# Attention and a bilinear feed-forward layer: the scaling of the second batch's sums of exponentials moves from VectorE to ScalarE

## The chip, the cores and the metric

The kernel runs on one core of a Trainium2 chip. The core has five engines that run their own queues of instructions in order and wait for one another through semaphores: TensorE (PE in the profile, with its weight loads as PEld), VectorE (DVE), ScalarE (ACT), GpSimd (POOL) and SyncE (SP), which here only issues DMAs. The metric is the time of one execution on the device in microseconds (us), lower is better. The median of three runs of the kernel before is 1006.17 us (1006.15 to 1007.19).

## The reference

Sliding-window attention over 8 batches, 8 heads, 576 positions and 64 channels per head is followed by a feed-forward layer that multiplies two projections with each other:

```python
scores = np.matmul(q, k.transpose(0, 1, 3, 2)) / np.sqrt(64)
bias = slopes[:, None, None] * (-np.abs(rel))        # rel = i - j
mask = (rel >= 0) & (rel < 128)
scores = np.where(mask, scores + bias, -1e9)
scores = scores - scores.max(axis=-1, keepdims=True)
attn = np.exp(scores)
attn = attn / (attn.sum(axis=-1, keepdims=True) + 1e-9)
x = (attn @ v)          # heads side by side: 4608 tokens x 512
out = ((x @ w_a) * (x @ w_b)) @ w_out      # 512 -> 1536 -> 512
```

All inputs and the output are float32.

## The kernel before

The float32 products are made of float16 ones: a matrix is scaled by a power of two and split into a high and a low float16 part, and three products (high by high, high by low, low by high) are added in PSUM. PE is therefore the engine with most of the work.

Attention goes by pairs of heads, four pairs to a batch, and a pair by nine blocks of 64 queries, which lie in four PSUM banks (`BANKS`). `scores` multiplies q and k of one bank on PE (L374 in the second batch, in plain float32; L378 in the later ones), adds the bias and takes the minimum on DVE (L382), and takes the exponential on ACT with its row sum (L383, into `sm`). `normalize` does this for the blocks that have been scored since the last call: it turns the sums into scaled reciprocals `rin` (one small instruction, L392 or L395, then the reciprocal on DVE, L396), and for each block multiplies the exponentials by `rin` and splits them into a high part on ACT (L399) and a low part on DVE (L400), both into `phl`. It is called twice for a pair, for 5 and 4 blocks or for 7 and 2. `transpose_probs` then transposes `phl` by a DMA that SP issues (L405), and `pv` multiplies it with v on PE (L501). ACT copies the result back over v (L414), and `split_x` (L435 on ACT, L436 on DVE) makes from it the float16 input `xs` of the feed-forward layer.

The first batch's attention has its own code (`first_attention`). The second batch's, `o.b == 1`, runs while PE does the first batch's feed-forward layer. From the third batch on, q and k are also scaled and split: squares on ACT (L321, with a row sum), the factor by way of DVE (L324, L336) and a small product on PE (`qtot`, L332), the split on ACT and DVE (L338, L339), then four DMAs on SP that lay the parts out (L347 to L350). The load of q and k of the pair after it (L311, L312) stands on SP behind these. There is one buffer for the loaded q and k, one for `phl` and one for the transposed probabilities `pT`.

The feed-forward layer of the first batch is `first_up` (the two projections, L836 on PE; copied by ACT at L783, multiplied by DVE at L785, split by ACT L829 and by DVE or POOL L830) and `first_down` (L812 on PE). `first_down` works in two halves of the tokens; each half adds up in four PSUM banks at a time, which ACT (L822) and DVE (L820) empty when it is complete, and the second half needs these banks. Five banks in all take turns. In the same time the weights are converted from float64: L131 and L133 on DVE, L130 on ACT and L135 on POOL, with squares on ACT (L141) and a sum over all partitions on PE (`wtot`, L101), after which ACT and DVE split the down weights (L230, L231).

What sets the order: the generators are woven together by `Pace` and `weave`, and a scheduler then orders the instructions of each engine by its own estimate of when each is ready, with some of them lifted by `high_priority`. SP's order is as written in the code everywhere. PE's is as written from the second batch's feed-forward layer on; in the first batch's it too comes from the scheduler. Once ordered, each engine takes its queue strictly from the front.

Of the kernel before, what the change touches and what calls it, by code (L numbers as in the profile page):

```python
# [17 lines left out]
AF = mybir.ActivationFunctionType  # L18
ALU = mybir.AluOpType
# [11 lines left out]
PSC = float(2.0**14)  # L31
# [15 lines left out]
def attention_then_bilinear_ffn(ctx: ExitStack, tc: tile.TileContext, qT, kT, vP, w_a, w_b, w_out, rel, slopes2, outT):  # L47
    nc = tc.nc
    vec, act, pe, pool, sp = nc.vector, nc.scalar, nc.tensor, nc.gpsimd, nc.sync
# [337 lines left out]
    def normalize(o):  # L387

        a, z = o.parts[0][0], o.n

        if o.b < 2:
            vec.tensor_scalar(out=o.rin[:, a:z], in0=o.sm[:, a:z], scalar1=1e-9, scalar2=1.0 / PSC, op0=ALU.add, op1=ALU.mult)  # L392
        else:

            act.activation(o.rin[:, a:z], o.sm[:, a:z], AF.Copy, scale=1.0 / PSC, bias=1e-9 / PSC)  # L395
        vec.reciprocal(o.rin[:, a:z], o.rin[:, a:z])  # L396
        for m, e, pc, w in o.parts:
            s = o.rin[:, m:m + 1]
            act.activation(phl[:, 0, pc:pc + w], e, AF.Copy, scale=s)  # L399
            vec.scalar_tensor_tensor(out=phl[:, 1, pc:pc + w], in0=e, scalar=s, in1=phl[:, 0, pc:pc + w], op0=ALU.mult, op1=ALU.subtract)  # L400
        o.parts = []
# [256 lines left out]
    def attention():  # L658
# [34 lines left out]
        for i in range(n + 1):  # L693
# [26 lines left out]
            if o and p != 2:  # L720
                with behind():
                    normalize(o)
# [7 lines left out]
            if two == 2 and p in (1, 3):  # L730
                if p == 2:
                    with behind():
                        normalize(o)
                scores(o, 3)
            yield i + 4 / 7
            if p == 2:
                prev.vhl = split_v(st, prev.p)
                if two == 1 or p not in (1, 3):
                    with behind():
                        normalize(o)  # L740
# [320 lines left out]
```

## Time and profile before

| | |
|---|---|
| median of the runs | 1006.17 us |
| the profiled execution's own time | 1006.95 us |
| its span in the trace | 1005.2 us |
| instructions | 23888 |
| PE idle or waiting, 100 to 200 us | 8.7 us |
| PE idle or waiting, 200 to 300 us | 2.7 us |
| DVE L396 | 56 instructions, from 66.9 to 860.7 us |

The span is what the trace covers; the execution's own time is some 1.8 us longer. The profile's page gives the busy time of each engine and the costliest groups of instructions. A line of the timeline gives start, duration, engine, line of the kernel, operation, output and inputs, and in brackets the idle time of the engine ahead of it with what ended that time. SPq stands for the issue of a DMA by SP.

### The profile page before, as it was taken

What the parts mean: (1) busy time and instruction counts of PE and PEld (TensorE: products, weight loads), DVE (VectorE), ACT (ScalarE), POOL (GpSimd) and SP (SyncE); (2) the same over time, 40 slices, a digit from 0 to 9 for tenths busy, and PEclk for the clock granted to TensorE, in tenths of its full rate; (3) what the DMA queues carried; (4) which work ended last, traced back from release to release, by engine and by line L of the source; (5) the groups of instructions that cost most, each with busy time, mean ns of one, the idle gap of its engine ahead of it and who ended that gap; (6) DMA issues with size and microseconds to landing.
All of it is one profiled execution on the core that took longest, in us unless ns stands there. A gap on an engine that the chain in (4) does not pass through costs nothing.

```text
span 1005.2 us, 23888 instructions
## 1 busy us (share of the span) xinstructions
PE 970.8 (97%) x9339; PEld 753.6 (75%) x9339; DVE 674.8 (67%) x1833; ACT 648.9 (65%) x1715; POOL 306.1 (30%) x345
## 2 busy tenths in 40 slices
PE   8789989999999999999999999999999999999998
PEld 5557656777777777777787777777777777777776
DVE  5888999557878566785768687666677576524530
ACT  7976779657767756767767767677666766413321
POOL 3533463104565321352226112220223022211100
PEclk9889999999999999999999999999999999999999
DMA  9317733564444442462624642474425632210001
GB/s 349 120 43 269 231 114 74 120 166 80 100 90 100 137 90 43 97 172 71 121 52 105 172 90 46 93 178 103 84 57 107 163 67 43 49 37 7 2 13 36
DMA packets 148433, 102.83 MB, mean 102 GB/s; under 512 B 120032, under 2 KB 128352, under 8 KB 147296
## 3 DMA queue, kind: packets, MB, share of 16 engines
q1 hardware_dynamic: 138816, 91.77, 37.2%
q10 hardware_dynamic: 9504, 9.54, 2.9%
q8 instruction: 73, 1.20, 0.5%
q14 instruction: 40, 0.33, 0.1%
HBM read 48.33 MB, written 9.44 MB: 57 GB/s over the span
## 4 chain that ended last, share of the span: by engine, by line
PE 70%; DVE 10%; ACT 4%; DMA 2%; issue 1%; POOL 1%; SPq 0%; ACTq 0%; DVEq 0%
PE dn_ps L932 19%; PE ch L836 19%; PE p L836 14%; PE up_ps L836 10%; PE x_ps L501 4%; PE sc_ps L378 3%; DVE phl L400 2%; PE dn_ps L812 2%; DMA v<-in_vP 1%; DVE t L382 1%; DVE xs L436 1%; ACT t L383 1%; DVE wup L150 1%; ACT phl L399 1%; DVE wup L257 1%
## 5 line engine op out<-in xcount | busy, mean ns | idle before, releaser
L836 PEld LDWEIGHTS <-wup 128*128 128x128 f16 x4224 | 409.1, 98 | 120.8 <-issue 14.3
L932 PE MATMUL dn_ps<-h,wdn 128*128 128x288 f16 x2016 | 254.3, 286 | 0.0
L932 PEld LDWEIGHTS <-wdn 128*128 128x128 f16 x2016 | 193.9, 98 | 51.7
L836 PE MATMUL ch<-xs,wup 128*128 128x288 f16 x1536 | 221.5, 286 | 0.8 <-ACT rc L861 0.6
L836 PE MATMUL up_ps<-xs,wup 128*128 128x288 f16 x1536 | 197.7, 288 | 5.8 <-DVE rc L785 4.2
L836 PE MATMUL p<-xs,wup 128*128 128x288 f16 x1152 | 172.6, 286 | 0.0
L891 POOL TENSOR_TENSOR rc<-rc,row 128x288 f32<-128x288 f32 x64 | 62.3, 974 | 278.8 <-DVE row L889 262.9
L400 DVE SCALAR_TENSOR_TENSOR phl<-t,rin,phl 128x192 f16<-128x192 f32 (+2 forms) x252 | 109.5, 474 | 19.0 <-ACT phl L399 18.8
L383 ACT ACTIVATE t<-t,mn 128x192 f32<-128x192 f32 (+2 forms) x252 | 107.2, 427 | 23.3 <-DVE mn L382 23.0
L829 ACT CAST h<-rc 128x576 f16<-128x576 f32 x96 | 64.2, 669 | 68.2 <-DVE rc L896 37.6
L399 ACT ACTIVATE phl<-t,rin 128x192 f16<-128x192 f32 (+2 forms) x252 | 88.7, 425 | 23.0 <-DMA pT<-phl 10.9
L830 DVE TENSOR_TENSOR h<-rc,h 128x576 f16<-128x576 f32 x90 | 71.1, 790 | 32.7 <-ACT h L829 32.0
L382 DVE CUSTOM_DVE_ANT_0 t<-sc_ps,bias,neg 128x192 f32<-128x192 f32 (+2 forms) x216 | 73.7, 389 | 7.8 <-PE sc_ps L378 7.7
L135 POOL TENSOR_TENSOR wup<-wup,wdn 128x512 int32<-128x512 int32 x36 | 54.6, 1539 | 44.6 <-DVE wup L133 14.6
L937 ACT ACTIVATE row<-dn_ps,oi 128x288 f32<-128x288 f32 x56 | 27.6, 494 | 56.7 <-PE dn_ps L932 56.5
L873 ACT ACTIVATE row<-ch,g 128x288 f32<-128x288 f32 x64 | 31.8, 497 | 50.1 <-PE ch L836 50.1
L436 DVE TENSOR_TENSOR xs<-v,xs 128x576 f16<-128x576 f32 x52 | 48.7, 950 | 21.7 <-ACT xs L435 21.5
L360 POOL TENSOR_SCALAR bias<-rel_sb,ninv,sl_sb 128x192 f32<-128x192 f32 x24 | 21.3, 887 | 123.5 <-DVE mn L382 123.5
L868 DVE TENSOR_TENSOR rc<-p,rc 128x288 f32<-128x288 f32 x64 | 29.1, 454 | 44.4 <-PE p L836 35.0
L896 DVE SCALAR_TENSOR_TENSOR rc<-rc,g,ch 128x288 f32<-128x288 f32 x64 | 32.6, 510 | 23.8 <-PE ch L836 23.6
L383 ACT ACTIVATION_READ_ACCUMULATOR t<-t,mn 128x1 f32 x252 | 47.7, 189 | 0.0
L430 POOL TENSOR_TENSOR xq<-xq,sq 128x576 bf16<-128x576 bf16 x22 | 29.6, 1345 | 56.8 <-ACT sq L429 56.7
(151 smaller groups left out, 1315.6 us busy)
## 6 DMA issues: line engine op xcount, KB each, us to landing
v<-in_vP SPq DMA_DIRECT2D x8, 1280.0 KB, 6.5
out<-row ACTq DMA_DIRECT2D x60, 144.0 KB, 1.8
qk<-in_qT SPq DMA_DIRECT2D x28, 288.0 KB, 3.9
qk<-in_kT SPq DMA_DIRECT2D x28, 288.0 KB, 4.4
wdn<-in_w_a SPq DMA_DIRECT2D x12, 512.0 KB, 4.5
wdn<-in_w_b SPq DMA_DIRECT2D x12, 512.0 KB, 5.6
wdn<-in_w_out SPq DMA_DIRECT2D x12, 512.0 KB, 4.3
qst<-qkh SPq DMA_DIRECT2D x24, 144.0 KB, 2.7
```

Of the source, the lines that this page charges most:

```text
L135: pool.tensor_tensor(out=t[:, m, :], in0=t[:, m, :], in1=low[:, m, :], op=ALU.add)
L382: vec.tensor_tensor_reduce(out=t[:, c:c + w], in0=ps[:, c:c + w], in1=o.bias[:, WIN - w:WIN], scale=-0.125 if o.b == 1 else o.neg, scalar= ...
L383: act.activation(t[:, c:c + w], t[:, c:c + w], AF.Exp, bias=o.mn[:, n:n + 1], scale=-1.0, accum_out=o.sm[:, n:n + 1])
L399: act.activation(phl[:, 0, pc:pc + w], e, AF.Copy, scale=s)
L400: vec.scalar_tensor_tensor(out=phl[:, 1, pc:pc + w], in0=e, scalar=s, in1=phl[:, 0, pc:pc + w], op0=ALU.mult, op1=ALU.subtract)
L436: vec.tensor_tensor(out=xs[:, n, 1, :, :], in0=src, in1=xs[:, n, 0, :, :], op=ALU.subtract)
L501: pe.matmul(xp[oc // 512][64 * h:64 * h + 64, o0:o0 + w], vt[0:rows, c:c + 64], probs(pt, rows, blocks, h), start=(n == 0 and first), stop ...
L829: act.copy(h[:, f, :, 0, :], hid)
L830: eng.tensor_tensor(out=h[:, f, :, 1, :], in0=hid, in1=h[:, f, :, 0, :], op=ALU.subtract)
L836: pe.matmul(ps[:, 0:HT], wup[:, a[0], a[1], wi, k, :], xs[:, b, xi, k, :], start=(first and n == 0), stop=(last and n == len(ks) - 1), ski ...
L891: pool.tensor_tensor(out=x0, in0=x0, in1=mid, op=ALU.mult)
L932: pe.matmul(ps[:, 0:HT], wdn[:, f, wi, e * P:(e + 1) * P], h[:, f, t, hi, :], start=(m == 0 and n == 0), stop=(m == NF - 1 and n == 2))
```

## The change

In `normalize` the branch for the first two batches goes. The second batch now scales its sums as the later ones do: ACT computes `sm / PSC + 1e-9 / PSC` in one instruction where DVE computed `(sm + 1e-9) / PSC`. (`normalize` is never called for batch 0.)

```diff
-        if o.b < 2:
-            vec.tensor_scalar(out=o.rin[:, a:z], in0=o.sm[:, a:z], scalar1=1e-9, scalar2=1.0 / PSC, op0=ALU.add, op1=ALU.mult)
-        else:
-
-            act.activation(o.rin[:, a:z], o.sm[:, a:z], AF.Copy, scale=1.0 / PSC, bias=1e-9 / PSC)
+
+        act.activation(o.rin[:, a:z], o.sm[:, a:z], AF.Copy, scale=1.0 / PSC, bias=1e-9 / PSC)
         vec.reciprocal(o.rin[:, a:z], o.rin[:, a:z])
```

The instructions are the same but for these eight. The order is not: from some 133 us on the scheduler lays out the rest of the first batch's feed-forward layer differently, up to about 215 us; SP's order stays as it was. In the changed file the lines behind the diff are 3 lower, so that L396, L399 and L400 read L393, L396 and L397, L414, L429 and L435 read L411, L426 and L432, and L783 and L829 read L780 and L826. Everywhere else in this text the lines are those of the kernel before.

On ACT, where the down weights are split (L230), the last two splits of the third pair of heads of the second batch (`phl`, L399 x2) stood right behind the twelfth L230:

```order
L230 ACTIVATE wdn<-wup,ratio 128x512 x11
L783 COPY rc<-up_ps 128x288
L230 ACTIVATE wdn<-wup,ratio 128x512
L399 ACTIVATE phl<-t,rin 128x192 x2
L414 ACTIVATE v<-x_ps 128x512
```

In the changed kernel, the place on ACT where they are now, thirteen instructions behind the last L230:

```order
L432 CAST xs<-v 128x576
L426 ACTIVATE sq<-v 128x576
L432 CAST xs<-v 128x576
L396 ACTIVATE phl<-t,rin 128x192 x2
L383 ACTIVATE t,sm<-t,mn 128x192 x2
L826 CAST h<-rc 128x2x288
L338 ACTIVATE qkh<-qk,own 128x1152
```

They have moved behind the second of two casts of x, and just ahead of the split of the third batch's first q and k (L338).

Next on ACT, a little later, the end of the fourth pair of the second batch: its last exponentials (L383 x2) and splits (L399 x4) stood ahead of the squares of the next loaded q and k (L321). Before:

```order
L414 ACTIVATE v<-x_ps 128x64
L429 ACTIVATE sq<-v 128x576
L383 ACTIVATE t,sm<-t,mn 128x192 x2
L399 ACTIVATE phl<-t,rin 128x192 x4
L321 ACTIVATE qkl,qs<-qk 128x1152
```

And in the changed kernel, the same place on ACT:

```order
L411 ACTIVATE v<-x_ps 128x64
L426 ACTIVATE sq<-v 128x576
L321 ACTIVATE qkl,qs<-qk 128x1152
L383 ACTIVATE t,sm<-t,mn 128x192 x2
L392 ACTIVATE rin<-sm 128x4
L396 ACTIVATE phl<-t,rin 128x192 x4
```

L321 is now ahead of them, with the added scaling (L392 here) among them.

The same place on DVE before, with the reciprocal and the low parts (L400) of that pair ahead of L324, which uses L321's sum, and then the first scores of the third batch:

```order
L396 RECIPROCAL rin<-rin 128x4
L400 SCALAR_TENSOR_TENSOR phl<-t,rin,phl 128x192 x4
L324 TENSOR_SCALAR both<-halves,qs 128x2
L382 ISA t,mn<-sc_ps,bias,neg 128x64
L382 ISA mn 128x1
```

In the changed kernel, DVE at the same place:

```order
L324 TENSOR_SCALAR both<-halves,qs 128x2
L393 RECIPROCAL rin<-rin 128x4
L397 SCALAR_TENSOR_TENSOR phl<-t,rin,phl 128x192
L382 ISA t,mn<-sc_ps,bias,neg 128x64
L382 ISA mn 128x1
L382 ISA t,mn<-sc_ps,bias,neg 128x128
L382 ISA mn 128x1
```

L324 now leads, and the four low parts are spread among the scores' instructions; on both engines the emptying of the down product's banks (L820, L822) still comes behind all of these.

## The prediction

> **What bounds the kernel now.** I read the page's busy shares first, then a table of stages, then the waits of PE.
>
> ```profile
> PE 970.8 (97%) x9339; PEld 753.6 (75%) x9339; DVE 674.8 (67%) x1833; ACT 648.9 (65%) x1715; POOL 306.1 (30%) x345
> ```
> ```profile
> 100.00:200.00 100.00, 91.31 (x864) 67.40 (x862) 87.22 (x211) 76.79 (x187) 40.66 (x32) 0.97 0.51 137
> 200.00:300.00 100.00, 97.34 (x961) 75.98 (x959) 70.63 (x192) 67.81 (x186) 41.90 (x57) 1.00 0.49 110
> 600.00:700.00 100.00, 100.00 (x1014) 79.03 (x1013) 66.44 (x208) 69.85 (x191) 22.53 (x20) 1.00 0.42 99
> ```
> The columns of the table are the stretch, its length, and the busy us of PE, PEld, DVE, ACT and POOL, then the clock granted to PE. From 200 us on PE is the limit. Between 100 and 200 us it is busy 91.3 us and DVE 87.2: there PE waits for the vector engines. The second batch's attention, which the change touches, runs in just that stage:
>
> ```profile
> L395 ACT ACTIVATE rin<-sm x48: 193/198/213, 193.2 to 860.3; 128x5 f32<-128x5 f32 x18, 128x4 f32<-128x4 f32 x18, 128x7 f32<-128x7 f32 x6, 128x2 f32<-128x2 f32 x6
> L392 DVE TENSOR_SCALAR rin<-sm x8: 155/162/172, 66.6 to 183.2; 128x5 f32<-128x5 f32 x3, 128x4 f32<-128x4 f32 x3, 128x7 f32<-128x7 f32 x1, 128x2 f32<-128x2 f32 x1
> ```
> Eight instructions, between 66.6 and 183.2 us. The waits of PE between 60 and 300 us, of which the change can reach these (total, times, longest):
>
> ```profile
> PE up_ps L836 <- DVE rc L785: 4.2, 2, 2.3
> PE wtot L101 <- ACT t L383: 1.7, 1, 1.7
> PE up_ps L836 <- ACT rc L783: 0.5, 1, 0.5
> ```
> Whatever PE loses before 215 us is not made up later, since it has no slack to catch up in.
>
> **The eight instructions themselves.** DVE loses 8 x 162 ns = 1.3 us of work, ACT gains 8 x 198 ns = 1.6 us. On DVE they are not even worth that much, since the next one overlaps:
>
> ```profile
> 133.18 0.16 DVE L392 TENSOR_SCALAR rin<-sm 128x4 f32<-128x4 f32 x1
> 133.25 0.50 DVE L785 SCALAR_TENSOR_TENSOR rc<-rc,g,up_ps 128x288 f32<-128x288 f32 x1
> 153.91 0.18 PE L101 MATMUL wtot<-c,ones 128*128 128x1 bf16 x1 [1.69 <-ACT t L383]
> 167.15 1.63 PE L836 MATMUL up_ps<-xs,wup 128*128 128x288 f16 x12 [0.49 <-ACT rc L783]
> ```
> The one at 133.18 costs 0.07 us before PE's releaser L785. I give DVE 0.2 us of lead at this place. It does not last by itself: PE stands at wtot (153.91) until POOL's additions, ACT's squares and DVE have finished the weights, so only an earlier end of that chain counts. I take 0.2 us there. The wait of 0.49 us at 167.15 is for the copy L783 behind eleven L230 on ACT; in the new order it stands behind nine, so I count it as gone. Together **-0.7 us** (bounds: 0, and 1.69 + 0.49 = -2.2). On ACT the extra time is hidden by its waits for POOL up to 153 us; without that cover it would cost 1.6 us at most.
>
> **The moved pair.** The change also makes the scheduler lay the rest of this stage out differently, and that I price higher. First, the last two splits (L399, L400) of the third pair of heads:
>
> ```profile
> 167.62 0.79 ACT L399 ACTIVATE phl<-t,rin 128x192 f16<-128x192 f32 x2
> 169.75 0.74 DVE L400 SCALAR_TENSOR_TENSOR phl<-t,rin,phl 128x192 f16<-128x192 f32 x2
> 170.56 4.85 SPq L405 DMA_TRANSPOSE pT<-phl  x1
> 173.06 0.67 ACT L435 CAST xs<-v 128x576 f16<-128x576 f32 x1
> 173.63 0.47 ACT L383 ACTIVATE t<-t,mn 128x192 f32<-128x192 f32 x1
> ```
> Before, they are done at 170.5 and the transpose leaves at 170.56. Now ACT does them after the second L435 of this place, which ends its turn at 173.63. ACT shows no idle from 158 us to there; without the pair (0.7 us) and with my lead it reaches them at about 172.8 and is done at 173.5. On DVE a split of x (L436, 0.75 us) and two L382 stand before and between the two L400, so the transpose leaves at **X = 175.0** (172.8 + 2.2). The bounds are 170.5, as before, and 176.7, if POOL's work beside them slows L436 and L400, as it does one L400 here:
>
> ```profile
> 134.53 1.28 POOL L830 TENSOR_TENSOR h<-rc,h 128x576 f16<-128x576 f32 x1 [1.83 <-ACT h L829]
> 134.86 1.17 DVE L400 SCALAR_TENSOR_TENSOR phl<-t,rin,phl 128x192 f16<-128x192 f32 x1
> ```
> 1.17 us beside POOL, against 0.74 for the pair at 169.75.
>
> **What hangs on X.** SP issues in order, so the layout of the next batch's q and k, which stands behind the transpose, waits for it, and the load of the pair after that waits for the layout:
>
> ```profile
> DMA to landing us min/median/max: 6.7/6.8/8.8
> ```
> ```profile
> 178.96 0.53 SPq L347 DMA_DIRECT2D qst<-qkh  x1
> 184.70 0.65 SPq L312 DMA_DIRECT2D qk<-in_kT  x1
> 189.03 1.16 ACT L321 ACTIVATE qkl<-qk 128x1152 bf16<-128x1152 f32 x1 [3.96 <-DMA qk<-in_kT]
> ```
> The first of these is how long a transpose takes from issue to landing. From L347 to L321 are 10.07 us. The transpose holds SP for 4.85 us, so L347 comes at 179.85 and L321 at 189.9, 0.9 us later than before. By itself that is little. But L321 now stands on ACT **ahead** of the last exponentials, the scaling and the last four splits of the fourth pair, which before used the time in which ACT waited for this load:
>
> ```profile
> 183.58 1.49 ACT L399 ACTIVATE phl<-t,rin 128x192 f16<-128x192 f32 x4 [0.45 <-DVE rin L396]
> 190.32 0.23 DVE L324 TENSOR_SCALAR both<-halves,qs 128x2 bf16<-128x2 f32 x1 [4.80 <-ACT qkl L321]
> 191.95 0.51 DVE L820 TENSOR_SCALAR row<-dn_ps,oi 128x288 f32<-128x288 f32 x1
> 192.83 0.48 ACT L822 ACTIVATE row<-dn_ps,oi 128x288 f32<-128x288 f32 x1
> ```
> Behind them in both queues stand L820 and L822, which empty PE's four banks of the first half of the down product. How long that block takes is seen at 205 us, where the same instructions follow each other:
>
> ```profile
> 204.93 0.46 ACT L383 ACTIVATE t<-t,mn 128x192 f32<-128x192 f32 x1 [1.78 <-DVE mn L382]
> 206.40 1.49 ACT L399 ACTIVATE phl<-t,rin 128x192 f16<-128x192 f32 x4 [0.25 <-DVE rin L396]
> ```
> 1.47 us from the first exponential to the splits. So: L321 with its sum 189.9 to 191.15; splits from 192.6; the first L400 on DVE done at 193.4; the next batch's three L382 (0.8 us) at 194.2; the rest of DVE's queue (three L400 and two L382, 2.1 us) at 196.3; L820 then; ACT's five exponentials and its first L822 at 196.8, the second L822 from 197.0 to 197.4.
>
> PE's side:
>
> ```profile
> 173.02 4.58 PE L812 MATMUL dn_ps<-h,wdn 128*128 128x288 f16 x36
> 177.53 1.62 PE L501 MATMUL x_ps<-pT,vhl 128*64 128x128 f16 x40
> 191.97 0.17 PE L332 MATMUL qtot<-both,ones 128*128 128x2 bf16 x1
> 192.82 0.27 PE L378 MATMUL sc_ps<-qkh,qst 128*64 128x192 f16 x2
> 193.36 3.47 PE L812 MATMUL dn_ps<-h,wdn 128*128 128x288 f16 x27
> ```
> The product with v (x_ps) moves behind 37 more of the down product (4.58 us for 36), to 182.2, less 0.7 of lead: 181.5. The transpose lands at 175.0 + 6.8 = 181.8: **+0.3 us**. PE then comes to the scores before 193.36 at about 192.4 and waits for the L382 that free their bank until 194.2 (1.8), comes to the second half's next bank at 194.8 and waits for L820 (1.5), and at the last bank for the second L822 (0.4): **+3.7 us**. With the 0.3 it grows by 1 us for each us of X from 171.0 on, so the bounds are 0 at X = 171.0 or less and 5.7 at 176.7. The next product with v needs a transpose that leaves behind these splits, at 195.9, and lands at 202.7, when PE comes to it at 202.2: **+0.4 us**.
>
> Sum: -0.7 + 0.3 + 3.7 + 0.4 = **+3.7 us**. The profiled execution took 1006.95 us (span 1005.2), which is 0.8 above the median of 1006.17; against its own time the sum is 1010.65, and on the median **1009.9 us**.
>
> **The rivals.**
>
> *The clock falls too.* After a gap PE may go on at half speed:
>
> ```profile
> 130.15:133.56 3.41, 1.35 (x12) 1.00 0.81 299
> 133.56:136.97 3.41, 3.17 (x14) 0.50 0.52 202
> 150.62:154.04 3.42, 1.73 (x17) 1.00 0.98 205
> ```
> With 1.35 of 3.41 us busy the clock was 0.50 for the next stretch, with 1.73 of 3.42 it stayed full. The new waits leave 1.4 to 1.8 us busy in such a stretch, so it can go either way. The price is half of 3.41 us, 1.7, less the 0.4 that PE would have waited anyway: +1.3, so 1011.2. [...]
>
> *The block is covered.* If the L400 pair is done between 171 and 173 us, L820 and L822 come about when PE needs them. Below X = 173.3 the whole is under +2 us: 1006 to 1008. For it: at X = 170.56 all of this was hidden. Against it: ACT's queue alone puts the pair behind 172.8.
>
> *Faster: the weights are ready earlier.* POOL now does its last six additions of the weight conversion in one run. If the last one is done before 150.5 us instead of 152.25, the whole wait at wtot (1.69) goes, and with the 0.49 behind it that is -2.2: 1004.0. It decides only if the block above is covered as well. Against it: these additions wait for DVE's L133, whose queue up to there holds the same work as before.
>
> *The change does not do what it says* is out: in the new order all eight L392 are gone from DVE and eight more L395 stand on ACT.
>
> **How the numbers follow.** Forecast, block not covered and clock full: 0.50, with a range of its own from 1008.0 to 1011.5. Half clock too: 0.17, 1010 to 1013. Covered: 0.24. Faster: 0.09. Some 0.2% (2 us) is what a measurement of this kernel can tell from no change. So slower 0.67, same 0.24, faster 0.09. The range leaves out the faster case and the worst of the second: 1005.2 to 1012.8.
>
> **What would show it.** In the trace of the changed kernel: ACT idle for several us ahead of an L321 near 190 us with the two L383 behind it; the transpose of the third pair near 175; PE waiting for L382, L820 and L822 between 192 and 198 us, some 3.7 us in all; the same waits as before after 215 us. It would be wrong if L321 starts before 187 us, or if PE's waits before 155 us have changed by more than 1 us.

## The result and the profile after

| | before | after |
|---|---|---|
| median of the runs (4 each, taken together) | 1006.57 us | 1019.12 us |
| lowest to highest | 1006.15 to 1007.19 | 1018.62 to 1019.95 |
| span of the profiled execution | 1005.2 us | 1017.4 us |

The ratio is 1.0123, with a 95% interval of 1.0111 to 1.0135: the change costs 12.55 us. Slower was forecast, but by 3.7 us, and the range ended at 1012.8. One later run of the kernel before, beside e5 to e7 below, took 1732 us at a granted clock of 0.70 and is left out of all figures.

The page of the changed kernel has PE's busy time 4.0 us *up* at a span 12.2 us longer; the table of stages below it shows where time is lost. Columns as before: stretch, length, busy us of PE, PEld, DVE, ACT, POOL, then the clock granted to PE.

```profile
PE 974.8 (96%) x9339; PEld 755.1 (74%) x9339; DVE 674.1 (66%) x1825; ACT 649.5 (64%) x1723; POOL 305.5 (30%) x345
```
```profile
100.00:200.00 100.00, 88.38 (x785) 63.68 (x785) 81.28 (x196) 73.78 (x186) 38.84 (x31) 0.94 0.43 118
200.00:300.00 100.00, 93.78 (x930) 73.13 (x929) 63.41 (x185) 63.83 (x177) 33.41 (x44) 0.97 0.53 112
600.00:700.00 100.00, 100.00 (x990) 78.25 (x988) 67.74 (x216) 69.46 (x199) 22.89 (x21) 1.00 0.47 111
```

Two things change: PE idles 2.9 us more between 100 and 200 us and 3.6 us more in the next 100, and its clock falls, from 0.97 to 0.94 and from 1.00 to 0.97. The later stage shown, 600 to 700 us, is as before. The same matmuls at half clock stay busy for longer, which is why the page can show more busy time (the 38 matmuls at 154.98 below, with the clock at 0.50 up to 157.46, took 6.03 us instead of 4.83).

The waits of PE between 60 and 300 us in the changed kernel (total, times, longest):

```profile
PE x_ps L498 <- DMA pT<-phl: 4.3, 2, 3.7
...
PE sc_ps L378 <- DVE mn L382: 2.6, 2, 1.8
PE wtot L101 <- DVE c L100: 2.0, 1, 2.0
PE dn_ps L809 <- DVE row L817: 1.3, 1, 1.3
...
PE x_ps L498 <- DVE vhl L296: 0.7, 1, 0.7
```

New are the first line (PE did not wait for a transpose before), 1.8 us of the second, and the last two; the very last, for the split of v, lies at 144.7 us. (Lines behind the diff are three lower in the changed kernel: L817 was L820.) The wait of 0.5 us for the copy of up_ps is gone, as forecast.

The timeline of PE in the changed kernel, at the places that differ:

```profile
153.65 0.18 PE L101 MATMUL wtot<-c,ones 128*128 128x1 bf16 x1 [1.99 <-DVE c L100]
...
154.98 6.03 PE L833 MATMUL up_ps<-xs,wup 128*128 128x288 f16 x38
160.94 1.65 PE L498 MATMUL x_ps<-pT,vhl 128*64 128x128 f16 x42
...
184.48 1.62 PE L498 MATMUL x_ps<-pT,vhl 128*64 128x128 f16 x40 [0.57 <-DMA pT<-phl]
...
193.90 0.17 PE L332 MATMUL qtot<-both,ones 128*128 128x2 bf16 x1
...
196.62 0.27 PE L378 MATMUL sc_ps<-qkh,qst 128*64 128x192 f16 x2 [1.80 <-DVE mn L382]
...
198.71 6.82 PE L809 MATMUL dn_ps<-h,wdn 128*128 128x288 f16 x42 [1.34 <-DVE row L817]
209.22 2.91 PE L498 MATMUL x_ps<-pT,vhl 128*64 128x128 f16 x42 [3.69 <-DMA pT<-phl]
...
213.15 0.27 PE L378 MATMUL sc_ps<-qkh,qst 128*64 128x192 f16 x2
```

And the first and last of these places in the kernel before, in the same view:

```profile
154.82 4.83 PE L836 MATMUL up_ps<-xs,wup 128*128 128x288 f16 x38
159.58 1.65 PE L501 MATMUL x_ps<-pT,vhl 128*64 128x128 f16 x42
...
201.46 0.27 PE L378 MATMUL sc_ps<-qkh,qst 128*64 128x192 f16 x2
```

The same 38 matmuls behind wtot took 6.03 us instead of 4.83, and x_ps of the second pair starts 1.36 us later (160.94 instead of 159.58). From qtot (193.90, before 191.97: 1.93 later) to the scores at 213.15 (before 201.46: 11.69 later) PE does the same work and loses 9.76 us: 1.80 + 1.34 + 3.69 = 6.83 us of waits, and 2.8 us of half clock (42 matmuls of the down product in 6.82 us, which take 5.3 at the rate of the 38 in 4.83 above, so 1.5; x_ps in 2.91 instead of 1.62, so 1.3); 0.1 is left over. So 1.9 us were lost ahead of 194 us, 9.8 in these 20 us, and 0.5 behind.

What feeds PE there, from the timelines of the other queues of the changed kernel:

```profile
173.36 1.68 POOL L427 TENSOR_TENSOR xq<-xq,sq 128x576 bf16<-128x576 bf16 x1 [1.07 <-ACT sq L426]
```
```profile
173.90 1.75 DVE L433 TENSOR_TENSOR xs<-v,xs 128x576 f16<-128x576 f32 x1
...
176.46 1.10 DVE L397 SCALAR_TENSOR_TENSOR phl<-t,rin,phl 128x192 f16<-128x192 f32 x1
```
```profile
177.62 4.83 SPq L402 DMA_TRANSPOSE pT<-phl  x1
...
198.29 6.06 SPq L402 DMA_TRANSPOSE pT<-phl  x1
```
```profile
173.73 0.82 ACT L396 ACTIVATE phl<-t,rin 128x192 f16<-128x192 f32 x2
...
192.23 1.17 ACT L321 ACTIVATE qkl<-qk 128x1152 bf16<-128x1152 f32 x1 [4.76 <-DMA qk<-in_kT]
...
194.84 1.49 ACT L396 ACTIVATE phl<-t,rin 128x192 f16<-128x192 f32 x4 [0.25 <-DVE rin L393]
```

The branch of work that the prediction followed is there: the transpose of the third pair leaves late (177.62), the load for L321 behind it, L321 makes ACT wait 4.76 us with the fourth pair's end behind it, and the fourth pair's transpose leaves at 198.29. Before, that one left at 185.59.

Its landing is the surprise. The DMAs issued between 184 and 212 us in the changed kernel (KB each, median us from issue to landing):

```profile
out<-row ACTq DMA_DIRECT2D x2, 144.0 KB, 5.4
out<-rc ACTq DMA_DIRECT2D x2, 144.0 KB, 8.4
pT<-phl SPq DMA_TRANSPOSE x1, 10.9
```

10.9 us, where 6.7 to 8.8 was all that the kernel before showed. It leaves just ahead of the four output writes of `first_down`'s first half. Before, these came 8 us after it (first write at 193.34).

### The profile page after: what moved, and what is told of

It is laid out like the page before. It is cut to its first block, busy times and chain, and to the rows that moved or that the text cites. A ratio compares the mean times of both kernels' runs of the same rounds, so it can differ in the third digit from the quotient of the medians.

```text
span 1017.4 us, 23889 instructions
## 1 busy us (share of the span) xinstructions
PE 974.8 (96%) x9339; PEld 755.1 (74%) x9339; DVE 674.1 (66%) x1825; ACT 649.5 (64%) x1723; POOL 305.5 (30%) x345
## 4 chain that ended last, share of the span: by engine, by line
PE 69%; DVE 14%; DMA 7%; ACT 6%; issue 2%; SPq 1%; ACTq 0%; DVEq 0%
PE dn_ps L929 19%; PE ch L833 18%; PE p L833 13%; PE up_ps L833 9%; PE x_ps L498 4%; PE sc_ps L378 3%; DMA v<-in_vP 3%; DVE phl L397 3%; DMA wdn<-in_w_b 2%; DVE t L382 1%; DVE wup L150 1%; DVE xs L433 1%; PE dn_ps L809 1%; DMA pT<-phl 1%; ACT phl L396 1%
## 5 line engine op out<-in xcount | busy, mean ns | idle before, releaser
L833 PEld LDWEIGHTS <-wup 128*128 128x128 f16 x4224 | 409.6, 98 | 121.7 <-issue 14.5
L833 PE MATMUL ch<-xs,wup 128*128 128x288 f16 x1536 | 221.5, 286 | 1.6 <-ACT rc L858 1.1
L833 PE MATMUL up_ps<-xs,wup 128*128 128x288 f16 x1536 | 198.7, 289 | 4.8 <-DVE rc L782 3.9
L833 PE MATMUL p<-xs,wup 128*128 128x288 f16 x1152 | 172.6, 286 | 0.0
L397 DVE SCALAR_TENSOR_TENSOR phl<-t,rin,phl 128x192 f16<-128x192 f32 (+2 forms) x252 | 110.2, 477 | 27.7 <-ACT phl L396 27.6
L383 ACT ACTIVATE t<-t,mn 128x192 f32<-128x192 f32 (+2 forms) x252 | 107.1, 427 | 19.5 <-DVE mn L382 19.1
L826 ACT CAST h<-rc 128x576 f16<-128x576 f32 x96 | 64.2, 669 | 71.9 <-DVE rc L893 37.4
L396 ACT ACTIVATE phl<-t,rin 128x192 f16<-128x192 f32 (+2 forms) x252 | 88.8, 425 | 31.2 <-DMA pT<-phl 21.1
L382 DVE CUSTOM_DVE_ANT_0 t<-sc_ps,bias,neg 128x192 f32<-128x192 f32 (+2 forms) x216 | 73.8, 390 | 7.7 <-PE sc_ps L378 7.5
L433 DVE TENSOR_TENSOR xs<-v,xs 128x576 f16<-128x576 f32 x52 | 49.5, 966 | 21.4 <-ACT xs L432 21.4
L498 PE MATMUL x_ps<-pT,vhl 128*64 128x128 f16 (+3 forms) x1176 | 47.4, 232 | 5.0 <-DMA pT<-phl 4.3
L498 PEld LDWEIGHTS <-vhl 128*64 128x64 f16 (+1 forms) x1176 | 43.7, 111 | 10.8 <-issue 4.4
```

What stands on the lines that cost most here:

```text
L382: vec.tensor_tensor_reduce(out=t[:, c:c + w], in0=ps[:, c:c + w], in1=o.bias[:, WIN - w:WIN], scale=-0.125 if o.b == 1 else o.neg, scalar= ...
L383: act.activation(t[:, c:c + w], t[:, c:c + w], AF.Exp, bias=o.mn[:, n:n + 1], scale=-1.0, accum_out=o.sm[:, n:n + 1])
L433: vec.tensor_tensor(out=xs[:, n, 1, :, :], in0=src, in1=xs[:, n, 0, :, :], op=ALU.subtract)
L498: pe.matmul(xp[oc // 512][64 * h:64 * h + 64, o0:o0 + w], vt[0:rows, c:c + 64], probs(pt, rows, blocks, h), start=(n == 0 and first), stop ...
L826: act.copy(h[:, f, :, 0, :], hid)
L833: pe.matmul(ps[:, 0:HT], wup[:, a[0], a[1], wi, k, :], xs[:, b, xi, k, :], start=(first and n == 0), stop=(last and n == len(ks) - 1), ski ...
```

## The experiments

The theory: the loss is the new order, and the one call that makes it is that of the third pair's second half (two blocks). Rivals: the eight instructions cost it on ACT; or the order at the second pair, before 160 us, does. A call is named below by pair and first block, (2, 7) for the one just named. The branch quoted is that of the kernel before: where it holds, DVE scales.

| run | what it is | us | ratio to before, 95% interval |
|---|---|---|---|
| e1 | six calls on ACT | 1008.19 | 1.0001, 0.9991 to 1.0010 |
| e2 | only (2, 7) on ACT | 1018.92 | 1.0108, 1.0091 to 1.0125 |
| e3 | only (1, 5) on ACT | 1010.79 | 1.0030, 1.0021 to 1.0039 |
| e4 | whole change, L321 back in its place | 1010.94 | 1.0033, 1.0022 to 1.0045 |
| e5 | whole change, four writes left out | 1016.49 | 1.0087, 1.0070 to 1.0104 |
| e6 | as e2, L321 back in its place | 1012.38 | 1.0043, 1.0028 to 1.0058 |
| e7 | all but (2, 7) on ACT | 1009.96 | 1.0021, 1.0012 to 1.0031 |

The kernel before took 1007.67 us beside e1 to e4 and 1008.0 beside e5 to e7, so the ratios are what to compare.

**e1: six scalings, old order.**

```diff
-        if o.b < 2:
+        if o.b < 2 and (o.p, a) not in ((0, 0), (0, 5), (1, 0), (2, 0), (3, 0), (3, 5)):
```

> Six of the eight scalings go to ScalarE, all but the second half of the second pair and the second half of the third; the order of the work on TensorE, GpSimd and SyncE stays that of before. Theory (the loss is the new order of the fourth pair's end and of the third pair's transpose): 1005.0 to 1007.5 us, no loss, and no 1-us stretch at half clock between 195 and 212 us. Rival (what the instructions cost on ScalarE, eighth by eighth of the 12.5 us): 1016 us, 9.4 more than before.

1.0001: no loss and no gain. The stretch from 195 to 215 us (PE busy, then its clock) in e1:

```profile
195.00:215.00 20.00, 19.52 (x205) 1.00 0.58 130
```

and in the changed kernel:

```profile
195.00:215.00 20.00, 13.35 (x121) 0.83 0.54 85
```

Three quarters of the instructions moved cost nothing that can be measured. The rival of their cost on ACT (1016) falls.

**e2: one scaling, that of the third pair's second half.**

```diff
-        if o.b < 2:
+        if o.b < 2 and (o.p, a) != (2, 7):
```

> One scaling of the eight goes to ScalarE, that of the third pair's second half; it alone brings the conversion of L321 ahead of the fourth pair's end and the third pair's last splits behind two copies. Theory (new order there): most of the loss, 1014 to 1019 us, with waits of PE for the reduction L382 and for pT of over 1.5 us each between 195 and 212 us. Rival (cost of the instructions): an eighth of it, 1008.1 us. Rival (the loss begins at the second pair, before 160 us): 1006 to 1008 us.

1.0108, some 10.9 us from one instruction of 0.2 us. PE in e2:

```profile
185.95 2.86 PE L501 MATMUL x_ps<-pT,vhl 128*64 128x128 f16 x40 [2.90 <-DMA pT<-phl]
...
198.86 0.27 PE L378 MATMUL sc_ps<-qkh,qst 128*64 128x192 f16 x2 [0.45 <-DVE mn L382]
...
209.23 2.73 PE L501 MATMUL x_ps<-pT,vhl 128*64 128x128 f16 x42 [4.47 <-DMA pT<-phl]
```

The time is as the theory had it, and so is the wait for the fourth pair's transpose; the wait for L382 is not (0.45 us where over 1.5 was expected), since here PE itself comes later, held by the third pair's transpose. In its place PE waits 1.32 us at 200.93 for L822.

**e3: one scaling, that of the second pair's second half.**

```diff
-        if o.b < 2:
+        if o.b < 2 and not ((o.p, a) == (1, 5)):
```

> One scaling of the eight goes to ScalarE, that of the second pair's second half; it alone changes the order at 130 to 145 us on ScalarE, GpSimd and TensorE, with the conversion of L321 left behind the fourth pair's end. Theory (new order at the fourth pair's end): 1005 to 1009 us. Rival (the new order of the second pair, whose waits lead to half clock and push later work into each other): 1012 us or more. Rival (cost of the instructions): 1008.1 us.

1.0030, 3 us: between the two theories, and above the 1009 to which the first one reached. The second pair's order has a price of its own, a quarter of the loss. Where PE loses it in e3:

```profile
146.66 2.29 PE L501 MATMUL x_ps<-pT,vhl 128*64 128x128 f16 x38 [2.28 <-DVE vhl L296]
...
155.63 0.18 PE L101 MATMUL wtot<-c,ones 128*128 128x1 bf16 x1 [0.49 <-DVE c L100]
```

This is not how the whole change loses it. Here the wait for the split of v is 2.28 us, not 0.70, with half clock behind it (the 38 matmuls take 1.56 us in the changed kernel); at wtot PE waits only 0.49 us, and the clock behind it is full. A wait of 1.33 us ahead of the third pair's x_ps (182.07) comes on top.

**e4: the whole change with L321 held back.** The squares for the third batch's second pair are issued behind the last split of the fourth pair. The diff is cut to the line that does it; `last_split[0]` holds the last high split (L396 here) that was issued:

```diff
-            with behind():
+            with tc.issue_after(last_split[0].ins) if i == NPAIR else behind():
                 nxt = squares(i + 1)
```

> The whole change, all eight scalings on ScalarE, with one constraint: the conversion of L321 for the next window of work is put behind the last split of the fourth pair, as it stood before. Theory (new order at the fourth pair's end): 1007.5 to 1011 us, the loss mostly gone, the wait of PE for the reduction L382 at 195 us gone and the fourth pair's transpose issued before 192 us, ahead of the output writes. Rival (cost of the instructions): 1019 us still. Rival (order of the second and third pair): 1016 to 1019 us.

1.0033 against 1.0123: 9 of the 12.4 us come back, at the upper end of what was expected. From 195 us on PE is as busy as in e1, at full clock. The same stretch and the fourth pair's transpose in e4:

```profile
195.00:215.00 20.00, 19.41 (x206) 1.00 0.62 142
```
```profile
192.12 5.09 SPq L402 DMA_TRANSPOSE pT<-phl  x1
```

The transpose leaves at 192.12, where it was expected before 192, and still ahead of the writes. What is left, 3.3 us, is close to e3's 3.0, but its trace is that of e7 (below), not that of e3.

**e5: the whole change without the first four output writes.**

```diff
-                act.dma_start(outT[e * P:(e + 1) * P, b * S + t * HT:b * S + (t + 1) * HT], o)
+                (b or t) and act.dma_start(outT[e * P:(e + 1) * P, b * S + t * HT:b * S + (t + 1) * HT], o)
```

> The whole change without the four output writes of the first half of the first batch (that part of the output stays empty); the order on every engine is that of the changed kernel. Theory (the fourth pair's transpose takes 10.9 us because the four writes are in flight with it): it lands within 7.5 us of its issue at about 198.3 us, PE's wait for it goes from 3.7 us to under 0.5, the half clock behind it (1.3 us) goes too, and the kernel takes 1014 us (1012.5 to 1015.5). Rival (the transpose is slow there for another reason, and the late issue alone decides): it lands after 10 us or more and the time stays at 1018 to 1020 us.

The transpose issued between 184 and 212 us in e5, and PE there:

```profile
pT<-phl SPq DMA_TRANSPOSE x1, 7.4
```
```profile
199.74 6.98 PE L809 MATMUL dn_ps<-h,wdn 128*128 128x288 f16 x42 [1.34 <-DVE row L817]
206.78 1.65 PE L498 MATMUL x_ps<-pT,vhl 128*64 128x128 f16 x42
```

Without the writes the transpose lands after 7.4 us, PE no longer waits for it, and x_ps runs at full clock. The time falls from 1.0123 to 1.0087 of before, 3.6 us, less than the 5 expected, and 1016.49 is 1.0 us above the range; the kernel before was 1.4 us slower beside this run than beside the result, which the range did not allow for. From the start of wtot to the end of this x_ps PE takes 5.2 us less than in the changed kernel (53.28 instead of 58.48), as expected. But e5 comes to wtot 1.5 us later (155.15 instead of 153.65) on the same order, so not by the writes. That the writes slow the transpose is shown; how they do is not.

**e6: only (2, 7), with L321 held back as in e4.** The diff is cut as there.

```diff
-        if o.b < 2:
+        if o.b < 2 and (o.p, a) != (2, 7):
-            with behind():
+            with tc.issue_after(last_split[0].ins) if i == NPAIR else behind():
```

> As the run with the third pair's scaling alone (1018.9 us), with the conversion of L321 put behind the fourth pair's last split again, where it stood before. Theory (two separate losses: the third pair's transpose, issued about 7 us later, costs about 4 us of PE by its wait and half clock; the conversion ahead of the fourth pair's end costs the other 8): 1012 us (1010.5 to 1013.5), with PE's wait for pT at 186 us still there and the fourth pair's transpose issued before 196 us. Rival (the conversion ahead is the whole of the loss): 1006.5 to 1009 us. Rival (the late transpose of the third pair is the whole of it): 1017 us or more.

1.0043, as the theory of two losses had it. Of e2's 10.9 us, 6.5 go when L321 is put back (1.0108 less 1.0043) and 4.3 stay. PE and SP in e6:

```profile
184.87 1.62 PE L501 MATMUL x_ps<-pT,vhl 128*64 128x128 f16 x40 [2.92 <-DMA pT<-phl]
```
```profile
191.51 5.52 SPq L405 DMA_TRANSPOSE pT<-phl  x1
```

Of the 4.3 us, the trace shows 2.92 as PE's wait for the third pair's late transpose; the rest is not placed. The split is rough: in e2 x_ps runs at half clock behind that wait (2.86 us), in e6 at full clock (1.62), and that is not L321's doing. Nor does it carry over to the whole change. There the transpose leaves sooner behind the second pair's x_ps than in e2 (16.7 us, not 18.1), PE comes to the third pair's later (23.0 us, not 22.0), and it waits only 0.57 us (0.56 in e4), so that e4 loses 3.3 us and not 3.0 and 4.3 together.

**e7: all but (2, 7).**

```diff
-        if o.b < 2:
+        if o.b < 2 and (o.p, a) == (2, 7):
```

> Seven of the eight scalings on ScalarE, that of the third pair's second half back on VectorE; the order on TensorE, ScalarE, GpSimd and SyncE is then that of the run with the second pair's scaling alone (1010.8 us). Theory (that one scaling's place decides over most of the loss of the whole change, the second pair's order over some 3 us): 1009 to 1011.5 us. Rival (the scalings add up on ScalarE, seven eighths of 12.5 us): 1017 us.

1.0021. Seven of the eight scalings moved cost 2 us, not 11. PE in e7, behind wtot:

```profile
155.15 0.18 PE L101 MATMUL wtot<-c,ones 128*128 128x1 bf16 x1 [1.99 <-DVE c L100]
...
156.49 6.03 PE L836 MATMUL up_ps<-xs,wup 128*128 128x288 f16 x38
```

The second pair's order shows the same trace here as in the whole change: a wait of 1.99 us at wtot, and half clock behind it. How long PE takes from its matmuls of L836 (L833) near 127 us, the last common point, to the second pair's x_ps prices it: 34.86 us here (127.59 to 162.45), 34.84 in the whole change (126.10 to 160.94), 34.85 in e4 and 34.86 in e5, against 32.19 before (127.39 to 159.58), 32.18 in e1, 32.20 in e2 and 32.17 in e6. That is 2.65 us. In e3 it is 33.21.

No version beats the kernel before: the best one, e1, cannot be told from it. One thing wasn't tried: extra matmuls in the waits, to price the half clock by itself. Extra matmuls at wtot change the order of several engines again, and that they would hold the clock is not shown. The clock's share is therefore read from the traces alone.

## Why the prediction was right in kind and wrong in size

| step of the prediction | forecast | measured |
|---|---|---|
| the eight instructions, all up to 160 us | -0.7 | +1.4 (2.65 by the new order, less a lead of 1.29 at 126 us) |
| third pair's x_ps waits for its transpose | +0.3 | +0.6 |
| the down product's banks (L382, L820, second L822) | +3.7 | +3.1 (1.80 + 1.34 + 0) |
| next x_ps waits for its transpose | +0.4 | +3.7 |
| half clock behind these waits | a rival, +1.3 | +2.8 |
| the rest | 0 | +0.6 |
| sum | +3.7 | +12.2 in the trace |

**The chain was right, its prices were not.** The pair moved behind the second cast of x, X late, L321 late and ahead, ACT idle in front of it, the banks emptied late: each is in the trace, and e4 and e6 show by its removal that L321's place is the larger part. But the wait for the banks, to which the prediction gave its whole +3.7 us, is 3.1 of the 12.2; most of the loss lies in terms that it put at 0.4 us or at nothing.

**"Next x_ps: +0.4 us" is the term that failed most.** It took 6.8 us for the landing of the fourth pair's transpose. With 6.8 it would have landed at 205.1, when PE came to it at 205.5: the forecast of no more than 0.4 would have held even though it left at 198.29 and not at 195.9. But a transpose that leaves 12.7 us later meets what leaves at that time, the output writes, and it took 10.9. The prediction had the row with the maximum of 8.8 us in front of it and asked of each engine, but not of the DMA queues, what else is under way at the new time. e5 shows this term: 3.6 us with the clock behind it.

**Half clock was put down as a rival at 0.17, all or nothing, and came three times.** Twice behind the new waits (1.5 + 1.3 us). The prediction reckoned with 1.4 to 1.8 us busy in such a stretch; there were 0.75 and 0.32. The third time is the first term of the table. Stretches of the changed kernel (stretch, length, PE busy, clock):

```profile
150.64:154.05 3.41, 1.42 (x14) 1.00 0.96 201
154.05:157.46 3.41, 3.41 (x19) 0.50 0.41 88
```
```profile
194.98:198.40 3.42, 0.75 (x9) 1.00 0.01 2
198.40:201.81 3.41, 3.10 (x14) 0.50 0.74 149
...
205.22:208.64 3.42, 0.32 (x3) 1.00 0.82 148
208.64:212.05 3.41, 2.83 (x42) 0.50 0.00 0
```

**"The eight instructions: -0.7" had the wrong sign.** The wait of 0.49 us went, as counted, but not its time: from the second pair's x_ps to qtot the same 338 matmuls keep PE busy for 32.38 us instead of 31.90, at full clock, and why stays open (it is most of the rest in the table). The start of wtot came 0.26 us earlier (153.65), PE came to it 0.56 us earlier (151.66 instead of 152.22, start less wait), and so it waited 1.99 us instead of 1.69. The lead isn't the change's: PE stood 1.29 us ahead already at 126 us, since at 66.9 us x_ps took 3.00 us instead of 3.88, and e5, on the same order, does not have it. In the 3.41 us up to 154.05 PE was busy 1.42 us, and the clock was 0.50 in the next 3.41; before, it was busy 1.73 of the 3.42 us up to 154.04, and the clock stayed at 1.00. The prediction showed that very row, with 1.35 busy and half clock beside it, and did not ask whether wtot would keep its 1.73. The 2.65 us agree with e7's 2.1 and e3's 3.0, though e3 loses them in another way.

**X was 177.62, not 175.0, and beyond the bound of 176.7.** L433 took 1.75 us and an L397 1.10 beside POOL, as the bound allowed for (0.75 and 0.41 us for the one ahead of each); ACT was also later than 172.8 at the splits (173.73). By the prediction's own rule of 1 us for each us of X that makes 2.6 us more. It did not show in the bank term, since PE was late as well: it came to the third pair's x_ps at 183.9 (184.48 less 0.57), not at 181.5. So the 3.1 us measured there is not a good forecast but two errors of opposite sign.

**The sign set for a failure was too coarse.** It asked whether PE's waits before 155 us change by more than 1 us. From 118 to 155 us they grew from 5.9 to 6.6 us, at wtot by 0.3, and that was enough: less the wait cost there than the clock behind it.

## What to carry to other kernels

When an edit makes a scheduler lay a stretch out anew, price each moved instruction, above all a load's first user that goes ahead of work which used to fill its wait: one instruction of 0.2 us in the wrong place cost 10.9 us, six others nothing that could be measured. For each transfer that is moved, look at what the DMA queues carry at the *new* time: beside four writes the transpose took 10.9 us to land, without them 7.4. And where a wait grows, read the granted clock behind it too: at wtot 1.99 us of waiting instead of 1.69 came with a clock of 0.50 behind it instead of 1.00, 1.2 us on the 38 matmuls there.

## What the runs showed of the hardware

**The same wait brought half clock in e2 and none in e6.** Both wait for the same product, e2 for 2.90 us (183.05 to 185.95) and e6 for 2.92 (181.95 to 184.87). In e2, the stretches there:

```profile
182.15:185.56 3.41, 0.90 (x8) 1.00 1.13 211
185.56:188.98 3.42, 3.03 (x45) 0.50 0.52 117
```

and in e6:

```profile
179.68:183.09 3.41, 2.27 (x19) 1.00 1.17 217
183.09:186.51 3.42, 1.64 (x44) 1.00 0.76 155
186.51:189.92 3.41, 3.41 (x33) 1.00 0.65 151
```

In e2 PE was busy 0.90 us in the stretch ahead, and the next has a clock of 0.50. In e6 the clock was 1.00 over the whole wait and behind it. At wtot a wait of 1.99 us in the changed kernel was followed by half clock, and one of 1.69 us in the kernel before was not. Nor does the busy time of the stretch ahead sort them all: in the kernel before, 1.73 of 3.42 us (up to 154.04) was followed by a clock of 1.00, and 1.88 of 3.41 us (10.68 to 14.09) by 0.50. So neither number alone tells here whether half clock follows, and what decides is not shown. The four executions of e6 took 1011.1 and 1011.6 us at granted clocks of 0.990 and 0.988, and 1013.2 and 1013.3 us at 0.986; only the first of them has a trace, and why they differ is not shown.

**The transpose by DMA took longer beside plain writes:** 10.9 us from issue to landing in the changed kernel, with four writes of 144 KB issued within 3 us behind it, and 7.4 in e5, without them. In e2, where they follow it too, PE's wait for it ended 10.0 us behind its issue (199.19 to 209.23). The writes took longer as well: two of them a median of 8.4 us, and 3.2 in the kernel before.

**DVE beside POOL.** In the kernel before, a small instruction on DVE took this long while POOL ran (172.67 to 177.62):

```profile
173.34 1.25 DVE L113 TENSOR_SCALAR r<-cl 128x2 int32<-128x2 int32 x1
```

and in the changed kernel, while POOL was idle (172.29 to 173.36):

```profile
172.30 0.17 DVE L113 TENSOR_SCALAR r<-cl 128x2 int32<-128x2 int32 x1
```

L114 and L336 went the same way, 0.77 and 1.23 us beside POOL against 0.17 and 0.15. The first parts of L382 did not: they took 0.34 and 0.35 us at 174.50 and 174.78, beside POOL, and 0.35 at 171.91, ahead of it. That POOL is the cause is read from the overlap in time, and wasn't tried by itself.
